# A chunked delta-rule attention beside two matmul layers: attention steps as one TensorE burst each

## The chip, the cores and the metric

The kernel runs on one core of one Trainium2 chip. Its time is the time of one launch in device microseconds (us), inputs and outputs in the chip's main memory. Five instruction queues work side by side: PE (TensorE, with the weight loads shown apart as PEld), DVE (VectorE), ACT (ScalarE), POOL (GpSimd) and SP (SyncE, which issues every data DMA here). Each queue keeps its written order.

## The reference

```python
def _attn_ref(q, k, v, beta):                # 4 x 8 heads, 768 positions, 48 wide
    k_n = k / (norm(k) + 1e-6)
    state = zeros(B, H, 48, 48)
    for t in range(768):
        y[t] = q[t] @ state
        v_old = state.T @ k_n[t]
        state = state + beta[t] * outer(k_n[t], v[t] - v_old)
def _moe_ref(x, w_in, w_out, a, b):          # x [3072, 384], w_in [384, 2048]
    h = x @ w_in
    P = a[0] + a[1]*h + a[2]*h**2 + a[3]*h**3
    Q = 1 + |b[0]| * |h| + |b[1]| * h**2
    return (P / (Q + 1e-6)) @ w_out
def _moe2_ref(x, w_in, w_out):
    return max(x @ w_in, 0)**2 @ w_out
```

The result is `_moe2_ref(_moe_ref(attention))`.

## The kernel before

The 768 positions are cut into 12 chunks of 64, times 4 batches: 48 chunk steps, eight to a group, six groups (`g` = 0 to 5 in the code, here group one to group six). Inside a chunk the recurrence is a triangular inverse, made once for a whole group by POOL or DVE and two rounds of small matmuls (`m1`, L626, and `m2`, L640); `m1` and `m2` read transfers that pass through DRAM (`td`, `nd`). Then each step n does, for all 8 heads of its batch:

- **k**: `kv`, k and state and q, into a PSUM tile H. Two copies with a mask (POOL, L759) give M; the DVE takes a part from `vn` (L764).
- **t**: `tv`, inverse times `vn`, into U; two copies put it into the tile X.
- **c3**: L780 and L781, the output Y; one copy into `xin`.
- **u**: `ku`, k_n times U, added to the state by the DVE (L798).
- **g**: `gram`, the Gram matrix of the step two groups on (groups two to four), one copy into `Gs`.

In the profile k, t, u and g all stand on L721 and are told apart by their operands: `X,kTc`, `vn,TT`, `X,kn`, `kTg`. Before, a step's work stands in three PE tasks (`first`, `rest`): k of step n with t of step n-1; then c3; then u with g.

Layer one has 96 units (six blocks of 512 tokens times 16). **A** (L921) is nine matmuls of a unit into one PSUM bank, held until the rational function (ACT L938, L939, L944, L945, POOL L941, DVE L942 to L948) has read it; **B** (L957) is three calls, six matmul instructions, into three accumulator banks. Layer two, with 96 units more, follows without attention. Counted from one, the attention of group two stands between the units of block one, that of group six between those of block five; block six has none. A block needs the output of the group of its number.

PSUM has 8 banks: 3 accumulators, a pool `h` of 3 for A, a pool `att` of 2 for attention. A planner sets the order: every task has an engine, a planned duration, a due time and its dependences; `Plan.play` lays them out by a list schedule, `Plan.late` sets due times from the end, eight rounds, and the best order is written out. The kernel on the chip has only that order and the waits that follow from the data.

```python
    acc = banks[0:3]
    PL.pool("h", banks[3:6])
    PL.pool("att", banks[6:8])
    pl = ("att",) if g else ("att", "h")
```

Of the kernel before, what the change touches and what calls it, by code (L numbers as in the profile page):

```python
# [242 lines left out]
def kernel(ctx, tc, kT, kS, qT, kn, vn, beta, par_in, w1, w2, outT):  # L243
    nc = tc.nc
    PL = Plan()
    add, slot = PL.add, PL.slot
# [56 lines left out]
    TN = at.tile([128, 8, NP, 32], F32, name="TN")  # L303
# [132 lines left out]
    def gload(n, due, nb=0):  # L436
        dma(128, lambda: slot["kg", n], kS[n], w=[("kg", n)], due=due - 5, nb=nb, alloc=(("kTg",), ("kg", n)))

    def gram(n):

        t, kt = ps(("G", n), [128, NP, C]), slot["kg", n]
        for p in range(NP):
            for j in range(2):
                r = kt[64 * j:64 * j + 48, p]
                yield t[64 * j:64 * j + 64, p], r, r

    def gstore(n, due):
        either(0.37, 0.36, lambda: (slot["Gs", n], ps(("G", n), [128, NP, C])), r=[("G", n)], w=[("Gs", n)], due=due,
            alloc=(("Gs",), ("Gs", n)), free=[("G", n)])
        dma(128, gs[n // 8][:, n % 8], lambda: slot["Gs", n], r=[("Gs", n)], w=[("gs", n)], due=due, free=[("Gs", n)])  # L450

    def attention(g):
# [81 lines left out]
        if g < 2:  # L534
            add("DVE", 2.0, lambda: V.transpose(Gb.rearrange("r q c -> r c q"), Tt.rearrange("p a b -> p b a")), r=["Tt"], w=GB, due=d1, lock=1)
            add("DVE", 2.0, lambda: V.transpose(DN.rearrange("r s p c -> r c (s p)"), Tt), r=["Tt"], w=["DN"], due=d1 + 1, lock=1)
        else:
            dma(512, td[g], Tt, r=["Tt"], w=[("td", g)], due=d1, lat=2.0)
            add("ACT", 2.05, lambda: A_.copy(Gb, Tt.rearrange("p a b -> p b a")), r=["Tt"], w=GB, due=d1)
        TTg = TT[g % 2]  # L540
        if g < 2:
# [8 lines left out]
        for i in (1, 0) if g > 1 else ():  # L550
            for j in range(2):
                o = 64 * j + 32 * i
                dma(128, TTv[o:o + 32, :, 32 * i:32 * i + 32], tdv[i, j], r=[("td", g)], w=[("TTx", g % 2, i, j)],
                    due=d1 + 2, lat=3.4, iss=0.6, after=[PL.last[wT[0]]] if wT[0] in PL.last else [])
        if g > 1:
            for j in range(2):
                dma(128, nd[g][j], Gb[64 * j:64 * j + 32], r=GB, w=[("nd", g, j)], due=d1 + 2)
                for hf in range(2):
                    x = 64 * j + 32 * hf
                    dma(64, TN[x:x + 32, 4 * hf:4 * hf + 4].rearrange("r s p c -> r (s p) c"), nd[g][j][16 * hf:16 * hf + 16].rearrange("q r c -> r q c"),  # L560
                        r=[("nd", g, j)], w=[("TN", hf, x)], due=d1 + 3, lat=3.2, iss=0.6)
                dma(64, TTv[64 * j:64 * j + 32, 16:32, 32:64], tdv[1, j][:, 16:32], r=[("td", g)], w=[("T", g % 2, 1, 64 * j)], due=d1 + 2, lat=3.2, iss=0.6)

# [139 lines left out]
        def ku(k):  # L703

            n = 8 * g + k
            x, t, kn_ = X[n % B], dv(n), KN[n // B % 2]
            for p in range(NP):
                yield t[64:112, p], kn_[0:64, n % B, p], x[0:64, 0, p, 64:112]
                yield t[0:48, p], kn_[64:128, n % B, p], x[64:128, 1, p, 64:112]

        def products(*gens):

            gens = list(gens)
            while gens:
                for q in list(gens):
                    for _ in range(2):
                        y = next(q, None)
                        if y is None:
                            gens.remove(q)
                            break  # L720
                        M.matmul(*y, start=True, stop=True)  # L721

        def yv(n):
            return slot["Y", n][:, 0:NP * C].rearrange("r (p t) -> r p t", p=NP)
# [39 lines left out]
                    V.tensor_tensor(v_[:, b], v_[:, b], ps(hk, [128, NP, 112])[:, :, 64:112], op=ALU.subtract)  # L764
                add("DVE", 0.38, cr, r=[hk], w=[("vn", cb, b)], due=due, free=[hk])

        def rest(k, due):
            n = 8 * g + k
            c, b = divmod(n, B)
            cb, x, uk, yk, dk = c % 2, X[b], ("U", n), ("Y", n), ("dS", n)  # L770
            for j in range(2):
                def uo(j=j):
                    o = 64 * j
                    return x[o:o + 64, j, :, 64:112], ps(uk, [128, NP, D])[o:o + 64]
                either(0.33, 0.33, uo, r=[uk], w=[("Us", b, j)], due=due, free=[uk], after=[PL.last["S", b]] if c == 0 else [])

            def c3():
                t = yv(n)
                for p in range(NP):
                    M.matmul(t[0:48, p], x[0:112, 0, p, 64:112], x[0:112, 0, p, 0:64], start=True, stop=True)  # L780
                    M.matmul(t[64:112, p], x[:, 1, p, 64:112], x[:, 1, p, 0:64], start=True, stop=True)  # L781
            xr = [(y, b, j) for y in ("M", "Us") for j in range(2)]
            add("PE", 0.62, c3, r=xr + [("q", b), ("q1", b), ("S", b)], w=[yk], due=due + 2, alloc=(pl, yk))
            m = n + 16 if 0 < g < NG - 2 else None
            if m:
                gload(m, due)
            add("PE", 0.55, lambda: products(ku(k), *([gram(m)] if m else [])), r=[("Us", b, 0), ("Us", b, 1), ("kn", cb), yk] + ([("kg", m)] if m else []),
                w=[dk] + ([("G", m)] if m else []), due=due + 3, alloc=[(pl, ("G", m))] if m else None, free=[("kg", m)] if m else [])
            if m:
                gstore(m, due + 4)  # L790
# [12 lines left out]
            if b == B - 1:  # L803
                t2 = CT * (c % 2)
                for j, o in ((0, 0), (1, 64)):
                    dma(48, xin[o + 48:o + 64, 0:NK, t2:t2 + CT], xin[o:o + 48, 3, t2:t2 + CT],
                        r=[("xin", c % 2, y) for y in range(B)], w=[("xin3", c % 2, j)], due=due + 7, iss=0.57)

        for k in range(8):
            dn = step_due(8 * g + k)  # L810
            head(k)
            if g:
                first(k, k - 1 if k else None, dn)
                middle(k, dn + 1)
                if k:
                    rest(k - 1, dn + 1)
            else:
# [4 lines left out]
        if g:  # L822
            first(None, 7, dn + 3)
            rest(7, dn + 4)

    def pload():
        SY.dma_start(par[:, 0:6], par_in)
# [276 lines left out]
```

## Time and profile before

| what | value |
|---|---|
| median of 3 runs | 1109.71 us (1107.1 to 1110.93) |
| the profiled execution | 1110.19 us, its span 1108.5 us |
| PE busy | 1057.7 us (95%), 10014 matmuls and as many weight loads |
| DVE, ACT, POOL busy | 703.4, 647.6, 401.2 us |
| layer one's first A | 103.5 us |
| first A of its last block | 626.0 us |

A row of a timeline gives the start, the time from the first start to the last end, the engine, the line, the operation, the tiles, the shape and how many instructions are merged. An idle time before it stands in brackets, with what ended it. A PE row's last instruction is counted to its own end, which the next row may overlap.

### The profile page before, as it was taken

To read this page: it belongs to the slowest core of one execution; us is meant where nothing else is said; L and a number is where in the kernel's file an instruction comes from. 1 tells how busy PE (TensorE), PEld (TensorE's weight loads), DVE (VectorE), ACT (ScalarE), POOL (GpSimd) and SP (SyncE) were. 2 spreads that over 40 slices of the span, in tenths; PEclk is the share of its full clock that TensorE was granted. 3 is DMA by queue.
4 is the path that set the end of the run, shared out by engine and by line. 5 is a ranking of instruction groups with operands and counts; after the bars stand their busy time and mean duration, and the time that the engine had idled before them with its cause. 6 is when DMAs were issued, how large, how long until landed. Compare 5 with 4: busy or idle time off the path is not lost.

```text
span 1108.5 us, 24471 instructions
## 1 busy us (share of the span) xinstructions
PE 1057.7 (95%) x10014; PEld 752.1 (68%) x10014; DVE 703.4 (63%) x1124; ACT 647.6 (58%) x1173; POOL 401.2 (36%) x540
## 2 busy tenths in 40 slices
PE   6588999799989999999999899999999999999998
PEld 5576665466656666666666555688888888888887
DVE  5658889888658768766777599994334343333432
ACT  5264788676767777677778588754333242333422
POOL 6104589569628844972233143551000000000000
PEclk7677899999999999999999999999999999999999
DMA  7455326741650174034010220720001010000000
GB/s 235 120 144 166 75 90 190 166 128 31 144 116 34 50 161 110 5 103 83 29 28 12 90 85 30 252 89 29 29 0 57 1 51 8 1 29 1 29 1 29
DMA packets 120544, 84.01 MB, mean 76 GB/s; under 512 B 88048, under 2 KB 105584, under 8 KB 120432
## 3 DMA queue, kind: packets, MB, share of 16 engines
q1 hardware_dynamic: 120432, 82.44, 26.8%
q8 instruction: 79, 1.29, 0.5%
q14 instruction: 33, 0.27, 0.1%
HBM read 63.41 MB, written 17.83 MB: 73 GB/s over the span
## 4 chain that ended last, share of the span: by engine, by line
PE 84%; DVE 6%; POOL 3%; issue 3%; DMA 3%; ACT 1%; SPq 1%; DVEq 0%; ACTq 0%; POOLq 0%
PE bank L921 33%; PE bank L957 19%; PE bank L983 6%; PE bank L981 6%; PE bank L982 6%; PE bank L721 6%; PE bank L780 2%; PE bank L640 1%; POOL Tt L508 1%; DMA X<-in_qT_dram 1%; PE bank L626 1%; POOL tmp L504 1%; POOL mem L941 1%; PE bank L585 1%; DVE tmp L495 1%
## 5 line engine op out<-in xcount | busy, mean ns | idle before, releaser
L921 PE MATMUL bank<-xh,A 128*128 128x512 f32 x1152 | 360.6, 394 | 1.1 <-POOL A L880 1.1
L957 PE MATMUL bank<-mem,B 128*128 128x512 f32 x576 | 278.7, 615 | 0.7 <-DVE mem L948 0.7
L921 PE MATMUL bank<-xl,A 128*128 128x512 f32 x576 | 256.5, 445 | 6.0 <-DVE mem L948 5.2
L921 PEld LDWEIGHTS bank<-xh,A 128*128 128x128 f32 x1152 | 218.2, 190 | 63.4 <-issue 15.1
L941 POOL TENSOR_TENSOR mem<-mem 128x512 f32<-128x512 f32 x96 | 129.1, 1344 | 202.4 <-ACT mem L939 201.9
L957 PEld LDWEIGHTS bank<-mem,B 128*128 128x128 f32 x576 | 104.3, 192 | 97.5 <-issue 84.3
L969 DVE SCALAR_TENSOR_TENSOR mem<-bank,mem 128x512 f32<-128x512 f32 x96 | 66.3, 690 | 151.3 <-ACT mem L968 151.1
L968 ACT ACTIVATE mem<-bank 128x512 f32<-128x512 f32 x96 | 57.4, 598 | 152.9 <-PE bank L921 151.0
L921 PEld LDWEIGHTS bank<-xl,A 128*128 128x128 f32 x576 | 109.1, 189 | 45.9 <-issue 15.5
L983 PE MATMUL bank<-gh,C 128*128 128x512 f32 x288 | 113.7, 395 | 0.0
L981 PE MATMUL bank<-gl,C 128*128 128x512 f32 x288 | 113.5, 394 | 0.0
L982 PE MATMUL bank<-gh,C 128*128 128x512 f32 x288 | 112.0, 389 | 0.0
L972 DVE TENSOR_TENSOR gl<-mem,gh 128x512 fp32r<-128x512 f32 x96 | 71.5, 745 | 63.3 <-ACT gh L971 63.2
L946 DVE SCALAR_TENSOR_TENSOR mem<-mem,par,bank 128x512 f32<-128x512 f32 x96 | 71.3, 743 | 53.4 <-ACT bank L945 53.2
L971 ACT CAST gh<-mem 128x512 fp32r<-128x512 f32 x96 | 59.6, 621 | 74.8 <-DVE mem L969 62.0
L944 ACT ACTIVATE mem<-mem,par 128x512 f32<-128x512 f32 x96 | 69.3, 722 | 36.0 <-POOL mem L941 35.2
L942 DVE TENSOR_TENSOR mem<-bank,mem 128x512 f32<-128x512 f32 x96 | 65.8, 685 | 31.6 <-ACT mem L347 30.8
L938 ACT ACTIVATE mem<-bank 128x512 f32<-128x512 f32 x96 | 57.1, 595 | 46.1 <-PE bank L921 41.2
L939 ACT ACTIVATE mem<-mem,par 128x512 f32<-128x512 f32 x96 | 78.1, 814 | 2.3
L508 POOL TENSOR_TENSOR Tt<-Tt,tmp 128x31 f32<-128x31 f32 (+15 forms) x124 | 72.4, 584 | 8.2
L943 DVE SCALAR_TENSOR_TENSOR mem<-mem,par,bank 128x512 f32<-128x512 f32 x96 | 71.6, 745 | 3.9 <-ACT mem L938 1.4
L347 ACT COPY X<-bank 64x192 f32<-64x192 f32 (+1 forms) x184 | 62.0, 338 | 18.3 <-DVE vn L764 9.7
(124 smaller groups left out, 1546.4 us busy)
## 6 DMA issues: line engine op xcount, KB each, us to landing
raw<-in_w_dram SPq DMA_DIRECT2D x18, 768.0 KB, 5.5
B<-in_w_dram SPq DMA_DIRECT2D x10, 768.0 KB, 4.8
kTg<-in_kS_dram SPq DMA_DIRECT2D x40, 128.0 KB, 3.3
gs<-Gs SPq DMA_DIRECT2D x40, 128.0 KB, 2.5
kTc<-in_kT_dram SPq DMA_DIRECT2D x40, 128.0 KB, 2.5
X<-in_qT_dram SPq DMA_DIRECT2D x96, 48.0 KB, 2.9
kn<-in_kn_dram SPq DMA_DIRECT2D x12, 384.0 KB, 4.1
vn<-in_vn_dram SPq DMA_DIRECT2D x12, 384.0 KB, 3.6
```

Source lines behind the costliest of these rows:

```text
L508: P_.tensor_tensor(Tt[:, 0:a, s + 1:32], Tt[:, 0:a, s + 1:32], tv, op=ALU.subtract)
L921: M.matmul(h, a, b, start=(k == 0 and m == 0), stop=(k == NK - 1 and m == 2))
L939: add("ACT", 0.83, lambda: A_.activation(b(), a(), AF.Identity, bias=s(4), scale=s(5)), r=[ak, "par"], w=[bk], due=due + 3.3, alloc=(("b", ...
L941: add("POOL", 1.32, lambda: P_.tensor_tensor(b(), b(), a(), op=ALU.mult), r=[ak], w=[bk], due=due + 4.2, lock=1)
L943: add("DVE", 0.75, lambda: V.scalar_tensor_tensor(c(), c(), s(1), h(), op0=ALU.add, op1=ALU.mult), r=[hk, "par"], w=[ck], due=due + 6.3)
L944: add("ACT", 0.72, lambda: A_.activation(a(), b(), AF.Ln, bias=s(6)), r=[bk, "par6"], w=[ak], due=due + 6)
L946: add("DVE", 0.75, lambda: V.scalar_tensor_tensor(c(), c(), s(0), h(), op0=ALU.add, op1=ALU.mult), r=[hk, "par"], w=[ck], due=due + 8)
L957: M.matmul(acc[d], Bw[j][:, 128 * d:128 * d + 128], slot[gk], start=(j == 0), stop=(j == NJ - 1))
L972: add("DVE", 0.72, lambda: V.tensor_tensor(gl(), b(), gh(), op=ALU.subtract), r=[bk, gk, "late"], w=[lk], due=due + 5, lock=1, alloc=(("gl ...
L981: M.matmul(acc[d], wh, gl, start=(j == 0), stop=False)
L982: M.matmul(acc[d], wl, gh, start=False, stop=False)
L983: M.matmul(acc[d], wh, gh, start=False, stop=(j == NJ - 1))
```

## The change

In groups two to six one task `burst(t)` does at once k of step t, t of step t-1, and c3 and u of step t-2 (and g for step t-1): ten bursts a group. H, U and Y may take banks of either pool, and g goes into the free part of U's bank. Group one keeps the old tasks. The planned times of the transfers behind the inverse are longer, which moves only the planned order.

```diff
-    def gram(n):
...
+    def gram(n, t=None):
...
-            dma(512, td[g], Tt, r=["Tt"], w=[("td", g)], due=d1, lat=2.0)
+            dma(512, td[g], Tt, r=["Tt"], w=[("td", g)], due=d1, lat=2.5)
...
-                    due=d1 + 2, lat=3.4, iss=0.6, after=[PL.last[wT[0]]] if wT[0] in PL.last else [])
+                    due=d1 + 2, lat=4.5, iss=0.6, after=[PL.last[wT[0]]] if wT[0] in PL.last else [])
...
+        def burst(t, due):
+            r, w, al, fr, dur = [], [], [], [], 0.0
+            k0, k1, k2 = (x if 0 <= x < 8 else None for x in (t, t - 1, t - 2))
+            m = 8 * g + k1 + 16 if k1 is not None and g < NG - 2 else None
+            if k2 is not None:
+                n, b = 8 * g + k2, k2 % B
+                r += cin(b) + [("kn", n // B % 2)]
+                w, al, dur = w + [("Y", n), ("dS", n)], al + [(("att", "h"), ("Y", n))], dur + 0.65
+            if k0 is not None:
+                n, b = 8 * g + k0, k0 % B
+                r += [("kc", n), ("q", b), ("q1", b), ("S", b)]
+                fr += [("kc", n)]
+                w, al = w + [("H", n)], al + [(("att", "h"), ("H", n))]
+            if k1 is not None:
+                n = 8 * g + k1
...
+                w, al = w + [("U", n)], al + [(("att", "h"), ("U", n))]
+            if m:
+                gload(m, due - 1)
+                r, w, fr = r + [("kg", m)], w + [("G", m)], fr + [("kg", m)]
+            def go():
+                if k2 is not None:
+                    c3(8 * g + k2)
+                products(*([kv(k0)] if k0 is not None else []), *([tv(k1)] if k1 is not None else []),
+                         *([ku(k2)] if k2 is not None else []), *([gram(m, slot["U", m - 16][:, NP * D:NP * (D + C)].rearrange("r (p c) -> r p c", p=NP))] if m else []))
+            q = max((0.76 if k0 is not None else 0) + (0.36 if k2 is not None else 0), (0.37 if k1 is not None else 0) + (0.44 if m else 0))
+            add("PE", 0.22 + dur + q, go, r=r, w=w, due=due, alloc=al, free=fr)
+            if m:
+                gstore(m, due + 2, ("U", m - 16))
...
+        for t in range(10 if g else 0):
+            dn = step_due(8 * g + t) if t < 8 else step_due(8 * g + 7) + 3 * (t - 7)
+            burst(t, dn)
+            if t < 8:
+                middle(t, dn + 1)
+            if 0 < t < 9:
+                ucopy(t - 1, dn + 1)
+            if t > 1:
+                result(t - 2, dn)
```

`ucopy` (two copies of U) and `result` (copy of Y, state add, loads of q) are the rest of the old `rest`, unchanged. PE in the middle of group four (unit 41 of layer one), before; X0 to X3 are the four batches' tiles, L957 is B, L921 is A:

```order
L921 MATMUL bank5_74<-xh2_98,A8_87 128x512 x2
L780 MATMUL bank6_75<-X0_107 48x64
L781 MATMUL bank6_75<-X0_107 48x64
...
L721 MATMUL bank6_75<-X0_107,kn0_128 48x48 x2
L721 MATMUL bank7_76<-kTg0_136 64x64 x2
...
L957 MATMUL bank0_69<-mem_102,B_95 128x512
L721 MATMUL bank7_76<-X2_109,kTc2_134 64x112 x2
L721 MATMUL bank6_75<-vn0_130,TT1_112 64x48 x2
...
L957 MATMUL bank1_70<-mem_102,B_95 128x512
L957 MATMUL bank2_71<-mem_102,B_95 128x512
L921 MATMUL bank3_72<-xl0_99,A9_88 128x512
```

The same place now (A is L966, B L1002, c3 L783 and L784, the others L724):

```order
L966 MATMUL bank5_74<-xh2_98,A8_87 128x512 x2
L783 MATMUL bank6_75<-X0_107 48x64
...
L724 MATMUL bank3_72<-X2_109,kTc2_134 64x112 x2
L724 MATMUL bank7_76<-vn0_130,TT1_112 64x48 x2
L724 MATMUL bank6_75<-X0_107,kn0_128 48x48 x2
L724 MATMUL bank7_76<-kTg1_137 64x64 x2
...
L1002 MATMUL bank0_69<-mem_102,B_95 128x512
L1002 MATMUL bank1_70<-mem_102,B_95 128x512
L1002 MATMUL bank2_71<-mem_102,B_95 128x512
L783 MATMUL bank3_72<-X1_108 48x64
```

Two stretches of small matmuls with a B call between them became one, the burst's third bank is bank 3 of A's pool, and the next burst writes that bank again three B calls later. ACT at that place, before (L347 is the copies; L938, L939, L944, L945 are the rational function):

```order
L347 COPY X2_109<-bank7_76 64x4x64 x2
L347 COPY X1_108<-bank6_75 64x4x48 x2
L944 ACTIVATE mem_102<-mem_102,par_77 128x512
L945 ACTIVATE bank5_74<-mem_102 128x512
L938 ACTIVATE mem_102<-bank3_72 128x512
L347 COPY xin_78<-bank7_76 112x4x64
L939 ACTIVATE mem_102<-mem_102,par_77 128x512
L347 COPY Gs1_139<-bank6_75 128x256
```

And now (L983 and L984 are what L938 and L939 were):

```order
L347 COPY X3_110<-bank7_76 64x4x64 x2
L347 COPY X2_109<-bank4_73 64x4x48 x2
L347 COPY Gs0_138<-bank4_73 128x256
L347 COPY xin_78<-bank3_72 112x4x64
L983 ACTIVATE mem_102<-bank4_73 128x512
L984 ACTIVATE mem_102<-mem_102,par_77 128x512
```

The six copies behind a burst now stand in one piece, with the next unit's first operation behind them.

## Rows read from the trace of the kernel before

**Rows 1.** The page: chain that ended last, by engine.
```profile
PE 84%; DVE 6%; POOL 3%; issue 3%; DMA 3%; ACT 1%; SPq 1%; DVEq 0%; ACTq 0%; POOLq 0%
```

**Rows 2.** Busy time by stretch; the first line names the columns.
```profile
core 0: us, PE busy (x) PEld busy (x) DVE busy (x) ACT busy (x) POOL busy (x), PEclk, DMA share, GB/s
141.00:212.00 71.00, 67.62 (x829) 41.69 (x821) 64.07 (x98) 56.95 (x110) 61.89 (x79) 1.00 0.54 156
526.00:626.00 100.00, 99.80 (x767) 60.58 (x765) 70.42 (x116) 68.73 (x126) 26.91 (x32) 1.00 0.09 28
```

**Rows 3.** PE timeline of one step of group three: kt, t, c3 and ug.
```profile
303.17 0.61 PE L921 MATMUL bank<-xh,A 128*128 128x512 f32 x2
303.72 0.31 PE L721 MATMUL bank<-X,kTc 48*64 48x112 f32 x2
...
304.63 1.98 PE L957 MATMUL bank<-mem,B 128*128 128x512 f32 x4
306.54 0.67 PE L721 MATMUL bank<-vn,TT 64*64 64x48 f32 x16
307.14 0.26 PE L780 MATMUL bank<-X 112*48 112x64 f32 x1
...
311.13 0.61 PE L921 MATMUL bank<-xh,A 128*128 128x512 f32 x2
311.68 0.26 PE L780 MATMUL bank<-X 112*48 112x64 f32 x1
...
312.26 0.25 PE L721 MATMUL bank<-X,kn 64*48 64x48 f32 x2
...
312.88 2.84 PE L957 MATMUL bank<-mem,B 128*128 128x512 f32 x6
```

**Rows 4.** PE timeline, group six: c3 and u without g.
```profile
580.12 0.61 PE L921 MATMUL bank<-xh,A 128*128 128x512 f32 x2
...
581.25 0.56 PE L721 MATMUL bank<-X,kn 64*48 64x48 f32 x16
581.74 1.12 PE L957 MATMUL bank<-mem,B 128*128 128x512 f32 x2
```

**Rows 5.** PE timeline: B with nothing before it; k alone, then B.
```profile
329.80 2.74 PE L957 MATMUL bank<-mem,B 128*128 128x512 f32 x6
...
334.53 0.98 PE L721 MATMUL bank<-X,kTc 48*64 48x112 f32 x16
335.44 2.84 PE L957 MATMUL bank<-mem,B 128*128 128x512 f32 x6
```

**Rows 6.** PE timeline, group three: around a c3 that stands alone.
```profile
246.43 0.61 PE L921 MATMUL bank<-xh,A 128*128 128x512 f32 x2
...
247.56 2.84 PE L957 MATMUL bank<-mem,B 128*128 128x512 f32 x6
```

**Rows 7.** Timeline of all engines behind a kt of group four.
```profile
381.03 1.13 PE L957 MATMUL bank<-mem,B 128*128 128x512 f32 x2
...
381.54 1.44 ACT L347 COPY X<-bank 64x256 f32<-64x256 f32 x4
381.60 0.80 PE L921 MATMUL bank<-xl,A 128*128 128x512 f32 x1
```

**Rows 8.** DVE timeline: the last operation on that unit's bank.
```profile
392.06 0.69 DVE L948 SCALAR_TENSOR_TENSOR mem<-bank,mem 128x512 f32<-128x512 f32 x1
```

**Rows 9.** PE's waits from 141 to 224 us: total, times, longest.
```profile
PE bank L721 <- ACT X L347: 2.0, 1, 2.0
PE bank L921 <- POOL A L880: 1.1, 2, 0.6
```

**Rows 10.** Chain of waits near the end of block one: start, us, what.
```profile
212.85 1.03 POOL A L880
```

**Rows 11.** PE timeline at the m2 of group four.
```profile
323.58 1.39 PE L640 MATMUL bank<-ws,TN 32*32 32x32 f32 x86 [3.02 <-issue]
```

**Rows 12.** The page's instruction queue: packets, MB, share.
```profile
q8 instruction: 79, 1.29, 0.5%
```

More of the change, by code (lines that the diff above doesn't have):

```diff
@@ L437, in gload @@
         dma(128, lambda: slot["kg", n], kS[n], w=[("kg", n)], due=due - 5, nb=nb, alloc=(("kTg",), ("kg", n)))
-    def gram(n):
-        t, kt = ps(("G", n), [128, NP, C]), slot["kg", n]
+    def gram(n, t=None):
+        t, kt = ps(("G", n), [128, NP, C]) if t is None else t, slot["kg", n]
         for p in range(NP):
@@ L445, in gram, with gstore @@
                 yield t[64 * j:64 * j + 64, p], r, r
-    def gstore(n, due):
-        either(0.37, 0.36, lambda: (slot["Gs", n], ps(("G", n), [128, NP, C])), r=[("G", n)], w=[("Gs", n)], due=due,
-            alloc=(("Gs",), ("Gs", n)), free=[("G", n)])
+    def gstore(n, due, u=None):
+        def go():
+            t = ps(("G", n), [128, NP, C]) if u is None else slot[u][:, NP * D:NP * (D + C)].rearrange("r (p c) -> r p c", p=NP)
+            return slot["Gs", n], t
+        either(0.37, 0.36, go, r=[("G", n)], w=[("Gs", n)], due=due,
+            alloc=(("Gs",), ("Gs", n)), free=[u or ("G", n)])
         dma(128, gs[n // 8][:, n % 8], lambda: slot["Gs", n], r=[("Gs", n)], w=[("gs", n)], due=due, free=[("Gs", n)])
@@ L553, in attention @@
                 dma(128, TTv[o:o + 32, :, 32 * i:32 * i + 32], tdv[i, j], r=[("td", g)], w=[("TTx", g % 2, i, j)],
-                    due=d1 + 2, lat=3.4, iss=0.6, after=[PL.last[wT[0]]] if wT[0] in PL.last else [])
+                    due=d1 + 2, lat=4.5, iss=0.6, after=[PL.last[wT[0]]] if wT[0] in PL.last else [])
         if g > 1:
             for j in range(2):
-                dma(128, nd[g][j], Gb[64 * j:64 * j + 32], r=GB, w=[("nd", g, j)], due=d1 + 2)
+                dma(128, nd[g][j], Gb[64 * j:64 * j + 32], r=GB, w=[("nd", g, j)], due=d1 + 2, lat=4.2)
                 for hf in range(2):
@@ L560, in attention @@
                     dma(64, TN[x:x + 32, 4 * hf:4 * hf + 4].rearrange("r s p c -> r (s p) c"), nd[g][j][16 * hf:16 * hf + 16].rearrange("q r c -> r q c"),
-                        r=[("nd", g, j)], w=[("TN", hf, x)], due=d1 + 3, lat=3.2, iss=0.6)
-                dma(64, TTv[64 * j:64 * j + 32, 16:32, 32:64], tdv[1, j][:, 16:32], r=[("td", g)], w=[("T", g % 2, 1, 64 * j)], due=d1 + 2, lat=3.2, iss=0.6)
+                        r=[("nd", g, j)], w=[("TN", hf, x)], due=d1 + 3, lat=5.0, iss=0.6)
+                dma(64, TTv[64 * j:64 * j + 32, 16:32, 32:64], tdv[1, j][:, 16:32], r=[("td", g)], w=[("T", g % 2, 1, 64 * j)], due=d1 + 2, lat=4.8, iss=0.6)
         for hf in range(2 if g < 2 else 0):
@@ L765, in middle, with ucopy @@
                 add("DVE", 0.38, cr, r=[hk], w=[("vn", cb, b)], due=due, free=[hk])
-        def rest(k, due):
+        def ucopy(k, due):
             n = 8 * g + k
             c, b = divmod(n, B)
-            cb, x, uk, yk, dk = c % 2, X[b], ("U", n), ("Y", n), ("dS", n)
+            x, uk = X[b], ("U", n)
             for j in range(2):
@@ L775, in rest, with c3, cin, result @@
                 either(0.33, 0.33, uo, r=[uk], w=[("Us", b, j)], due=due, free=[uk], after=[PL.last["S", b]] if c == 0 else [])
[L777 to L790, printed above, removed]
+        def c3(n):
+            t, x = yv(n), X[n % B]
+            for p in range(NP):
+                M.matmul(t[0:48, p], x[0:112, 0, p, 64:112], x[0:112, 0, p, 0:64], start=True, stop=True)
+                M.matmul(t[64:112, p], x[:, 1, p, 64:112], x[:, 1, p, 0:64], start=True, stop=True)
+        def cin(b):
+            return [(y, b, j) for y in ("M", "Us") for j in range(2)] + [("q", b), ("q1", b), ("S", b)]
+        def result(k, due):
+            n = 8 * g + k
+            c, b = divmod(n, B)
+            x, yk, dk = X[b], ("Y", n), ("dS", n)
             t = CT * (c % 2) + C * b
@@ L807, in rest @@
                         r=[("xin", c % 2, y) for y in range(B)], w=[("xin3", c % 2, j)], due=due + 7, iss=0.57)
+        def rest(k, due):
+            n = 8 * g + k
+            c, b = divmod(n, B)
+            yk, dk = ("Y", n), ("dS", n)
+            ucopy(k, due)
+            add("PE", 0.62, lambda: c3(n), r=cin(b), w=[yk], due=due + 2, alloc=(pl, yk))
+            add("PE", 0.55, lambda: products(ku(k)), r=[("Us", b, 0), ("Us", b, 1), ("kn", c % 2), yk], w=[dk], due=due + 3)
+            result(k, due)
@@ new lines, in burst, with go @@
+        def burst(t, due):
[13 more added lines that the diff above has]
+                n = 8 * g + k1
+                r += [("T", g % 2, k1 // 4, o) for o in (0, 64)] + [("vn", n // B % 2, k1 % B)]
+                r += [("TTx", g % 2, i, j) for i in range(2) for j in range(2)] + ([("TT", g % 2)] if g < 2 else [])
+                w, al = w + [("U", n)], al + [(("att", "h"), ("U", n))]
+            if m:
+                gload(m, due - 1)
+                r, w, fr = r + [("kg", m)], w + [("G", m)], fr + [("kg", m)]
+            def go():
+                if k2 is not None:
[6 more added lines that the diff above has]
+                gstore(m, due + 2, ("U", m - 16))
@@ L809, in attention @@
         for k in range(8):
-            dn = step_due(8 * g + k)
             head(k)
[L812 to L817, printed above, removed]
+            if not g:
+                dn = step_due(8 * g + k)
                 first(k, None, dn)
@@ L821, in attention @@
                 rest(k, dn + 4)
-        if g:
-            first(None, 7, dn + 3)
-            rest(7, dn + 4)
+        for t in range(10 if g else 0):
[7 more added lines that the diff above has]
+                result(t - 2, dn)
     def pload():
```

## The prediction

> **What bounds the kernel now.** First I read the chain of waits: PE carries 84% of it [rows 1]. Then the busy times by stretch. While group six's attention runs (526 to 626 us) PE is busy 99.80 of 100 us and no other engine over 71, so there a microsecond off PE is a microsecond off the end. Between 141 and 212 us, in block one, it is less clear: PE 67.62, but DVE 64.07 and POOL 61.89 of 71 us, because the first layer's weights are prepared there [rows 2]. Then the PE timeline, which shows what small matmuls cost between the large ones; then ACT and DVE behind a step, since the new order asks them to be quicker.
>
> **PE work, before.** Large matmuls of A follow each other at 0.23 us, so a row of two ends its share 0.46 us after its start. From the A row at 303.17 to the B row at 304.63 are 1.46 us; less 0.46 the stretch of k and t costs 1.00 [rows 3]. k alone costs as much: 334.53 to 335.44 is 0.91 from its first matmul to B, and 303.72 to 304.63 is 0.91 too [rows 3, 5]. So t goes beside k for nothing: they use different lanes (k: rows of one half of the array into columns of the other; t: the same half). u shares k's lane, g shares t's. c3 with u and g costs 1.75 - 0.46 = 1.29 [rows 3]; without g 1.62 - 0.46 = 1.16 [rows 4]. c3 alone costs 1.13 - 0.46 = 0.67 [rows 6]; u with g apart 0.62 from first matmul to B, and about 0.09 ahead of it, 0.71 [rows 3]. t ahead of a c3 takes 0.60 [rows 3]. After every stretch the six B instructions take 2.84 instead of 2.74 [rows 5]: 0.10 more per stretch, which I add to each.
>
> A group with g, eight steps: k 1.10, seven kt at 1.10, eight c3+u+g at 1.39, one t 0.60: 20.5 us. Without g (groups five and six): 1.10 + 7.70 + 8 x 1.26 + 0.60 = 19.5.
>
> **PE work, now.** A full burst is c3 and then four kinds in two lanes. Ahead of it 0.09 (311.13 + 0.46 to 311.68); c3 and the step to the next kind 0.58 (311.68 to 312.26) [rows 3]. The longer lane is k then u. The sixteen k take 0.98 [rows 5]; the last one is 0.26 long, so it started at 0.72, and with one spacing of 0.10 the lane is held 0.82; 0.09 more until B. The sixteen u take 0.56 [rows 4], 0.21 of it the last one's: held 0.40. Lane: 0.82 + 0.40 + 0.09 = 1.31. The other lane, t and g, is 0.51 + 0.53 + 0.09 = 1.13 by the same way [rows 3] and hides. Burst: 0.09 + 0.58 + 1.31 + 0.10 = 2.08, with or without g. Bounds: if the lanes only pair as they did before (k beside t, then u beside g) 2.21; if nothing overlaps beyond before, the two old stretches, 2.49 (2.36 without g).
>
> Ten bursts of a group with g: k 1.10; k+t+g 1.32; six full 12.5; c3+t+u+g 1.90; c3+u 1.26: 18.1, so 2.4 less, three times: -7.3. Without g: 1.10 + 1.10 + 12.5 + 1.37 + 1.26 = 17.3, so 2.2 less, twice: -4.4. At five places the order before sets c3 and u further apart (0.77 + 0.81 against 1.39, so 0.2 each); these go: -1.0. PE work: **-12.7 us**, with 2.49 for a burst -2.
>
> **New waits.** Before, a kt had an A or two B calls behind it before its U was needed, and M another stretch more. Now the next burst needs at once the two copies of U, the DVE part of `vn`, and three banks, which the burst before has just filled. Behind the kt that ends at 381.03, ACT starts its four copies at 381.54 and ends at 382.98 [rows 7]: 1.95 us. The new order leaves between two bursts mostly an A and a B or more (2.9 us), or three B calls (2.57: three times 0.86, from [rows 5]), but at five places two B calls or one (1.7 or 0.9). There it is 0.3 us late and once 1.1: some 2 us. With only two banks left to A during the bursts, the next wait is for the rational function: A's start at 381.60 to L948's end at 392.75 is 11.15 us of holding a bank, with copies of a step in between [rows 7, 8]. In group four the new order comes back to the same bank after two A, two bursts and three B calls, 10.8 us: 0.4 late; groups three and six have similar places, some 1.5 us together. Sum **+3.5 us**. Below, zero (the copies may be split with the DVE, which had 30% free); above, if ACT's six copies stand in front of the rational function everywhere, 0.4 at each of 45 gaps, +18.
>
> The Trainium skill's page "TensorEngine Tiling (Array Packing)", section PSUM Bottleneck, speaks against the change: packing speeds up TensorE and not the emptying of PSUM, so the copies may become the bound, and it wants ScalarE and VectorE both on them. By it the +18 would be due; the row of four copies, 1.95 us against gaps of mostly 2.6 or more, bears it out only at the tight places.
>
> **Block one.** PE waits there 3.1 us for a copy and for weights [rows 9]; the last weight's POOL part ends at 213.88 [rows 10], and PE can't pass it, whatever it saves. The DVE has 7 of 71 us free [rows 2]. The order also puts one A of A's first three behind more filler, since a bank of `h` is taken early by H. I take -0.5 for all of this beside the PE work; bounds -4.6 (all of PE's waits and the late unit gone) and +4 (the 3.5 us of PE work of this group saved for nothing).
>
> **Nothing else.** The longer planned times issue no transfer and add no wait; they move `m1` and `m2`, which in the rows are held by no transfer. From the last block on the order is the same on every engine, so what block five gains reaches the end whole.
>
> The sum: -12.7 + 3.5 - 0.5 = -9.7. The profiled execution took 1110.19 us, 0.5 over the median of the runs shown: 1110.2 - 9.7 = **1100.5 us**.
>
> **Rivals.**
> 1. The waits don't come and block one gives its waits back: -12.7 - 4.6 = -17.3, 1093. For: the planner's order already leaves most gaps longer than the copies. Against: the tight places, and DVE in block one.
> 2. Nothing gained, by instruction loading. PE's instructions come in packets of 1.29 MB / 79 [rows 12], for 10014 matmuls and as many weight loads 254 each. In m2 of group four PE stands 3.02 us on "issue" [rows 11], with 256 instructions of m1 just behind it. A full burst is 160 instructions; 254 take at the tightest a burst, two B calls and a good half of the next, 4.8 us, against about 2.7 us in m1 and m2. If a packet needs more than that (3.02 + 2.7 = 5.7), ten places wait 0.9: +9, 1108 or so with the other terms. Against: before, a step's 128 to 160 instructions in 7 us never waited so. The Trainium skill's page "Runtime: NRT & Kernel Launch", section Instruction fetch mechanics, has this loading hidden behind the issue of instructions, so by it this rival is nil; the 3.02 us in m2 say that here it isn't always.
> 3. Slower: the emptying of the banks becomes the bound. Place: between two full bursts; each of 45 gaps waits on the last of the six copies, because an operation of the rational function (0.6 to 0.8 us) stands before them on ACT. Price per gap 0.4: +18, 1110.2 - 12.7 + 18 - 0.5 = 1115. It decides from 0.3 us a gap, where the gain is eaten. For: the order puts six copies in a piece and the next unit's first operation behind them, so A's banks come free later too. Against: in rows 2 ACT has 31 of 100 us free.
> 4. The burst doesn't overlap more than the old pairs did (2.49): -2 + 3.5 - 0.5 = +1, 1111. Against: the equal 0.91 of k alone and k with t.
>
> **How the numbers follow.** Forecast 0.58 (1095 to 1106), rival one 0.18, two 0.11, three 0.09, four 0.04. A run of this kernel tells 0.3%, 3.3 us, from no change. Faster holds the forecast, rival one and a quarter of rival two: 0.79. Same: the rest of two, part of three and four: 0.12. Slower: the rest, 0.09. The range takes rival one in and most of two, 1090 to 1110.
>
> **What would show it.** Full bursts from first matmul to the next large one near 1.9 us; 2.3 or more and the lanes are wrong. PE waits in groups three to six on ACT or DVE of some 3 us; 10 or more and rival three is on. Any "issue" stop inside a burst speaks for rival two. The last block's first A should come at about 616 us instead of 626.0. If the end moves less than that A does, something behind it took the gain back.

## The result and the profile after

The changed kernel takes 1095.84 us (1091.49 to 1099.99, 4 runs) where the kernel before took 1108.4 on the same chip: ratio 0.988 (95% interval 0.984 to 0.992), some 13 us less. The forecast was 1100.5, 9.7 us less than the profiled execution before. A second set of runs (first experiment) gave 0.988 again (0.985 to 0.990). The profiled execution is the fastest of the four: 1091.49 us, its span 1089.8.

The chain that ended last, by engine, from the page of the changed kernel, against [rows 1]:

```profile
PE 76%; DVE 9%; POOL 5%; ACT 3%; issue 3%; DMA 2%; SPq 2%; DVEq 0%; POOLq 0%; ACTq 0%
```

PE still carries it, with less than before. Busy time while group six's attention runs, with the columns of [rows 2]:

```profile
509.00:607.00 98.00, 97.89 (x766) 60.67 (x765) 69.33 (x116) 69.90 (x127) 26.89 (x32) 1.00 0.10 29
```

As in [rows 2] PE is full and no other engine above 72%, so work taken off PE is still worth its length there. Now one full burst of group three on PE, between two B calls (L783 is c3, L724 the other kinds, L1002 is B):

```profile
252.72 1.98 PE L1002 MATMUL bank<-mem,B 128*128 128x512 f32 x4
254.63 0.26 PE L783 MATMUL bank<-X 112*48 112x64 f32 x1
...
255.22 0.31 PE L724 MATMUL bank<-X,kTc 48*64 48x112 f32 x2
255.23 0.32 PE L724 MATMUL bank<-vn,TT 64*64 64x48 f32 x4
...
255.38 0.29 PE L724 MATMUL bank<-kTg 48*64 48x64 f32 x3
255.46 0.20 PE L724 MATMUL bank<-X,kn 64*48 64x48 f32 x1
...
256.35 0.26 PE L724 MATMUL bank<-X,kn 64*48 64x48 f32 x4
256.54 1.13 PE L1002 MATMUL bank<-mem,B 128*128 128x512 f32 x2
```

k and t, then g and u, begin within 0.25 us of each other and all are through 1.32 us after the first of them (255.22 to 256.54). From c3's first matmul to the next B are 1.91 us; with the 0.09 ahead of it the stretch costs 2.00, and the B instructions behind it take the same 0.10 more as in [rows 5] (0.53 us from the first B's start to the second's, where it is 0.43 without a stretch ahead). The forecast had 2.08 in all, the trace 2.10.

The last block's first A, 626.0 us before, on PE's timeline:

```profile
607.42 0.79 PE L966 MATMUL bank<-xl,A 128*128 128x512 f32 x1
```

It comes 18.6 us sooner, and the end 18.7 (1108.5 less 1089.8): from there on nothing is gained or lost. As the profiled execution is the fastest of the four, these 18.7 are more than the 12.6 of the medians. Where those 18.6 come from, by the first A of each block (103.5, 224.2, 327.3, 427.6, 525.9 and 626.0 us before; 102.5, 214.1, 314.1, 413.6, 509.6 and 607.4 now): 1.0 ahead of layer one, 9.1 in block one, 8.5 in blocks two to five. PE's waits in blocks two to five (total, times, longest, us), first the kernel before:

```profile
PE bank L640 <- issue: 4.5, 3, 3.0
PE bank L957 <- DVE mem L948: 0.7, 3, 0.3
PE bank L721 <- ACT X L347: 0.2, 1, 0.2
```

and the changed kernel:

```profile
PE bank L643 <- ACT ws L347: 4.4, 2, 2.3
PE bank L966 <- DVE xl L950: 1.3, 2, 0.7
PE bank L643 <- issue: 1.1, 1, 1.1
PE bank L966 <- DVE mem L993: 0.8, 1, 0.8
PE bank L1002 <- DVE mem L993: 0.6, 2, 0.5
```

No burst waits for a copy. What is new: m2 (L643) waits for the copy of m1's result, 2.3 and 2.1 us. The timeline of all engines at the first of the two says why:

```profile
308.96 0.35 ACT L476 ACTIVATE nby<-Gb,tiny 128x32 f32<-128x32 f32 x1 [3.09 <-DMA Gb<-gs]
...
310.84 0.59 ACT L347 ACTIVATE ws<-bank 128x512 f32<-128x512 f32 x1
...
311.49 1.29 PE L643 MATMUL bank<-ws,TN 32*32 32x32 f32 x128 [2.29 <-ACT ws L347]
```

ACT stands 3.09 us on a load for the next group's inverse (`Gb` from `gs`); the rational function and the copy `ws` queue behind it, and PE behind the copy.

### The profile page after: what moved, and what is told of

Its sections match the earlier page's. It is cut to its first block, busy times and chain, and to the rows that moved or that the text cites. A ratio compares the mean times of both kernels' runs of the same rounds, so it can differ in the third digit from the quotient of the medians.

```text
span 1089.8 us, 24429 instructions
## 1 busy us (share of the span) xinstructions
PE 1037.7 (95%) x10022; PEld 748.8 (69%) x10022; DVE 700.5 (64%) x1122; ACT 645.8 (59%) x1175; POOL 400.0 (37%) x540
## 4 chain that ended last, share of the span: by engine, by line
PE 76%; DVE 9%; POOL 5%; ACT 3%; issue 3%; DMA 2%; SPq 2%; DVEq 0%; POOLq 0%; ACTq 0%
PE bank L966 31%; PE bank L1002 16%; PE bank L1028 6%; PE bank L1026 6%; PE bank L1027 6%; PE bank L724 5%; SPq L332 2%; PE bank L783 2%; POOL Tt L511 2%; POOL tmp L507 2%; POOL mem L986 1%; DVE raw L910 1%; DMA kTg<-in_kS_dram 1%; DVE mem L993 1%; DVE mem L987 1%
## 5 line engine op out<-in xcount | busy, mean ns | idle before, releaser
L966 PE MATMUL bank<-xh,A 128*128 128x512 f32 x1152 | 358.2, 392 | 0.9 <-POOL A L925 0.9
L1002 PE MATMUL bank<-mem,B 128*128 128x512 f32 x576 | 271.5, 605 | 0.6 <-DVE mem L993 0.6
L966 PE MATMUL bank<-xl,A 128*128 128x512 f32 x576 | 254.8, 442 | 8.5 <-DVE mem L993 6.7
L966 PEld LDWEIGHTS bank<-xh,A 128*128 128x128 f32 x1152 | 217.3, 189 | 61.1 <-issue 14.5
L1002 PEld LDWEIGHTS bank<-mem,B 128*128 128x128 f32 x576 | 106.0, 191 | 99.4 <-issue 86.8
L966 PEld LDWEIGHTS bank<-xl,A 128*128 128x128 f32 x576 | 108.6, 189 | 53.4 <-issue 12.7
L1028 PE MATMUL bank<-gh,C 128*128 128x512 f32 x288 | 113.8, 395 | 0.0
L983 ACT ACTIVATE mem<-bank 128x512 f32<-128x512 f32 x96 | 56.9, 592 | 44.8 <-PE bank L966 39.0
L984 ACT ACTIVATE mem<-mem,par 128x512 f32<-128x512 f32 x96 | 78.0, 813 | 2.4
L347 ACT COPY X<-bank 64x256 f32<-64x256 f32 (+1 forms) x186 | 62.6, 339 | 20.2 <-DVE vn L767 9.6
L511 POOL TENSOR_TENSOR Tt<-Tt,tmp 128x31 f32<-128x31 f32 (+15 forms) x124 | 69.9, 563 | 8.3
```

The source lines that it names most:

```text
L511: P_.tensor_tensor(Tt[:, 0:a, s + 1:32], Tt[:, 0:a, s + 1:32], tv, op=ALU.subtract)
L966: M.matmul(h, a, b, start=(k == 0 and m == 0), stop=(k == NK - 1 and m == 2))
L984: add("ACT", 0.83, lambda: A_.activation(b(), a(), AF.Identity, bias=s(4), scale=s(5)), r=[ak, "par"], w=[bk], due=due + 3.3, alloc=(("b", ...
L1002: M.matmul(acc[d], Bw[j][:, 128 * d:128 * d + 128], slot[gk], start=(j == 0), stop=(j == NJ - 1))
L1028: M.matmul(acc[d], wh, gh, start=False, stop=(j == NJ - 1))
```

## The experiments

All were timed beside the kernel before, and each ratio is to that kernel on the same chip. "Block one" below is the time from its first A to that of block two, "two to five" from there to the first A of the last block, each from the profiled execution. The fifth column is the time lost at half clock within block one: the sum over 2 us windows of the window times (1 - granted clock). It is what the lower clock cost only if PE would not have waited instead. Columns four to six come from one execution of each kernel.

| kernel | median us | ratio (95% interval) | block one | of it half clock | two to five |
|---|---|---|---|---|---|
| before (first trace) | 1109.71 | 1 | 120.7 | 7.7 | 401.8 |
| changed (first trace) | 1095.84 | 0.988 (0.984-0.992) | 111.6 | 1.7 | 393.3 |
| e1 changed, again | 1096.48 | 0.988 (0.985-0.990) | 112.2 | 2.0 | 395.5 |
| e2 longer times alone | 1113.12 | 1.003 (1.001-1.005) | 122.2 | 7.5 | 400.2 |
| e3 bursts, old times | 1103.06 | 0.993 (0.990-0.996) | 121.5 | 2.7 | 391.9 |
| e4 bursts from group three | 1107.05 | 0.998 (0.996-1.000) | 120.1 | 3.8 | 395.8 |
| e5 lanes in pairs | 1097.13 | 0.988 (0.986-0.990) | 113.8 | 1.7 | 394.0 |
| e6 c3 last | 1097.82 | 0.988 (0.986-0.990) | 113.4 | 1.7 | 393.2 |
| e7 copies on ACT | 1097.36 | 0.988 (0.986-0.990) | 114.1 | 2.2 | 395.0 |
| e8 two banks for A | 1126.9 | 1.016 (1.013-1.018) | 121.1 | 9.4 | 396.3 |
| e9 Gram load 7.0 | 1105.68 | 0.996 (0.994-0.997) | 118.9 | 8.5 | 394.7 |
| e10 Gram load 5.0 | 1106.8 | 0.996 (0.995-0.998) | 120.6 | 5.1 | 394.3 |
| e11 before, Gram load 7.0 | 1112.32 | 1.002 (1.000-1.004) | 116.2 | 1.7 | 403.0 |
| e12 c3 twice | 1098.73 | 0.991 (0.988-0.994) | 113.0 | 0.4 | 394.9 |

**e1, the changed kernel again** (no edit).

> The changed kernel once more, for the spread of its times and for the same-chip comparison. Theory one (the time comes from PE work: a step's two stretches of small matmuls, some 1.1 + 1.3 to 1.4 us, became one of 2.10): ratio 0.985 to 0.992; a full burst again 2.00 us plus 0.10, and the blocks two to five of layer one again within 1.5 us of 100.0, 99.5, 96.0 and 97.8 us. Theory two (a good part of the 18.7 us by which its first trace was shorter is TensorE's granted clock, which that trace shows at half speed for some 6 us less of the first 640 us than the trace of before): the span differs from 1089.8 us by the time spent at half clock in this trace.

Ratio 0.988, the full burst 2.00 us again, blocks two to five 100.9, 100.4, 96.4 and 97.8 us. Theory one holds. Theory two holds from layer one on at most: the four blocks are 2.2 us longer than in the first trace, with 5.1 us lost at half clock against 1.7 there. Over the whole execution it fails: the mean granted clock is higher here (0.974 against 0.970), and the span is 5.4 us longer, 2.5 of them ahead of layer one, whose first A comes at 105.0 instead of 102.5.

**e2, the longer planned times alone**, in the kernel before (the five `lat` of the diff):

```diff
-            dma(512, td[g], Tt, r=["Tt"], w=[("td", g)], due=d1, lat=2.0)
+            dma(512, td[g], Tt, r=["Tt"], w=[("td", g)], due=d1, lat=2.5)
```

> The kernel before, with the longer planned times of the transfers and nothing else. Theory one (the bursts make the gain, the planned times none): 1105 to 1111 us, ratio 0.997 to 1.003. Rival (the order around the inverse makes it: m1 and m2 moved to where their operands are ready): 1104 us or less, ratio 0.996 or less, and less waiting at m1 and m2 (7.8 us of gaps in the trace of before).

1113.12, two us above theory one's range and slightly slower than the kernel before (1.003). The rival, 1104 or less, falls; the planned times by themselves gain nothing.

**e3, the bursts with the old planned times** (the same five undone in the changed kernel):

```diff
-            dma(512, td[g], Tt, r=["Tt"], w=[("td", g)], due=d1, lat=2.5)
+            dma(512, td[g], Tt, r=["Tt"], w=[("td", g)], due=d1, lat=2.0)
```

> The changed kernel with the planned transfer times of before. Theory one: within 3 us of the changed kernel, 1093 to 1099 us. Rival (the longer times matter with bursts, where m1 and m2 find fewer stretches to stand between): 4 us or more above the changed kernel, with waits of m1 or m2 on a transfer or a copy that it doesn't have.

The rival's number came, 6.6 us above e1, but not at m1 or m2: blocks two to five are the shortest of all, 391.9, and block one is 121.5. The longest of PE's waits there:

```profile
PE bank L966 <- DVE xl L950: 7.2, 1, 7.2
```

and on ACT, ahead of the copies that the next block's first A needs:

```profile
221.41 0.35 ACT L476 ACTIVATE nby<-Gb,tiny 128x32 f32<-128x32 f32 x1 [6.97 <-DMA Gb<-gs]
```

The load that makes m2 late in the changed kernel makes the whole next block late here. With the longer times SP begins to issue the four transfers of that load 101.9 us after layer one's first A (102.5 to 204.4 us), with the old ones 107.2 us after it (105.8 to 213.0). In blocks two to five m2 waits for `ws` here too, with the old planned times:

```profile
PE bank L643 <- ACT ws L347: 3.7, 2, 2.4
```

So that wait comes with the order of the bursts and not with the longer times; e2, old tasks with the longer times, has none there.

**e4, bursts from group three on** (group two by the old tasks):

```diff
+        def rest0(k, due):
...
+            if g == 1:
...
+                first(k, k - 1 if k else None, dn)
...
-        for t in range(10 if g else 0):
+        for t in range(10 if g > 1 else 0):
```

(`rest0` is the old `rest`.)

> Bursts in groups three to six alone; group two, between the units of block one, keeps the old tasks. Theory one with block one's own gain real (in the traces block one became 9.1 us shorter, of which some 3 us are half clock; 5.2 us attention stretches and 1.3 us waits): 5 to 7 us above the changed kernel, 1100 to 1103 us, blocks two to five as in the changed kernel. Rival (block one is held by the preparing of the weights, so PE work there is worth nothing, and its 9 us were clock and luck): within 2 us of the changed kernel.

1107.05, above both ranges: block one is back at 120.1 (3.8 of it half clock), and blocks two to five keep their gain but for 2.5 us against the first trace of the changed kernel (0.3 against e1). The rival falls. But the order of block one is new here too, so this doesn't tell the old tasks from the new order.

**e5, the lanes in pairs**:

```diff
-                products(*([kv(k0)] if k0 is not None else []), *([tv(k1)] if k1 is not None else []),
-                         *([ku(k2)] if k2 is not None else []), ...
+                products(*([kv(k0)] if k0 is not None else []), *([tv(k1)] if k1 is not None else []))
+                products(*([ku(k2)] if k2 is not None else []), ...
```

> The changed kernel with the same order of tasks; inside a burst k and t are issued to their end and only then u and g, instead of all four in turn. Theory one (part of the gain is that u starts in k's lane and g in t's without a common stop): a full burst 2.11 instead of 2.00 us, 30 of them, 3.5 us in all: 1098 to 1102 us, the four last attention blocks 0.6 to 0.9 us longer each. Rival (the whole gain is that two stretches became one, with one entry and one 0.10 us behind it): 2.00 to 2.03 us a burst and the changed kernel's time, 1094 to 1098 us.

The rival holds: 1097.13 us, and the burst, on PE's timeline:

```profile
260.22 0.26 PE L783 MATMUL bank<-X 112*48 112x64 f32 x1
...
261.53 0.26 PE L724 MATMUL bank<-X,kTc 48*64 48x112 f32 x2
261.55 0.22 PE L724 MATMUL bank<-kTg 48*64 48x64 f32 x2
261.62 0.21 PE L724 MATMUL bank<-X,kn 64*48 64x48 f32 x2
...
262.13 1.13 PE L1002 MATMUL bank<-mem,B 128*128 128x512 f32 x2
```

1.91 us from c3 to B, as with all four in turn: g starts beside the last k, without a stop. So the order in which the four kinds are issued is worth nothing; what gains is that k and t, and c3, u and g, are one stretch: 1.10 + 1.40 = 2.50 became 2.10. By the prediction's terms, 0.28 of these 0.40 are one way in (0.09), one way out (0.09) and one 0.10 less. The other 0.12 would be that g, longer than u, no longer stands alone at the end; no run takes these apart.

**e6, c3 at the end of the burst**:

```diff
             def go():
-                if k2 is not None:
-                    c3(8 * g + k2)
                 products(...)
+                if k2 is not None:
+                    c3(8 * g + k2)
```

> The changed kernel with the same order of tasks; c3 stands at the end of a burst instead of its head, so H and U are ready some 0.6 us sooner and Y later. Theory one (in blocks two to five no burst waits for a copy: the traces show no gap ahead of one there): the same PE work, blocks two to five as before, block one 0 to 3 us shorter (bursts wait there 1.8 to 3.2 us): 1093 to 1098 us. Rival three of the prediction (the copies behind a burst set the pace): 4 us or more gained, 1092 or less.

1097.82, the same time, blocks two to five 393.2. That H and U are ready 0.6 us sooner is worth nothing; block one is not shorter either, so theory one holds but for its hope for block one, and rival three's 1092 or less did not come.

**e7, every copy of a burst on ACT**:

```diff
-                either(0.38, 0.36, co, r=[hk], w=[("M", b, j)], due=due, free=[hk])
+                (cact if g else either)(0.38, 0.36, co, r=[hk], w=[("M", b, j)], due=due, free=[hk])
```

(the copies of U and Y likewise; `cact` adds the copy to ACT alone).

> The changed kernel with every copy of M, U and Y of groups two to six on ACT; the planner may no longer give some to the DVE, and lays out its order anew. Rival three of the prediction (emptying the banks is the bound where ACT does it all): 0.4 us at each of 45 gaps, 1108 to 1116 us, with PE waits on ACT ahead of bursts in blocks two to five. Theory one (the gaps between bursts are longer than the copies): 1094 to 1104 us, no such waits in blocks two to five; what changes is block one, whose order is new.

1097.36. PE's waits in blocks two to five (L969 is A, L1005 B and L724 the small matmuls here; the 2.0 in the first row is ahead of the first A of block two):

```profile
PE bank L969 <- DVE xl L953: 2.8, 2, 2.0
PE bank L1005 <- DVE mem L996: 2.5, 2, 1.6
PE bank L643 <- ACT ws L347: 2.5, 1, 2.5
PE bank L643 <- issue: 1.4, 2, 0.7
PE bank L724 <- ACT xin L752: 0.2, 1, 0.2
```

A burst waits for a copy once, for 0.2 us. Rival three of the prediction falls.

**e8, three banks for attention and two for A**:

```diff
-    PL.pool("h", banks[3:6])
-    PL.pool("att", banks[6:8])
+    PL.pool("h", banks[3:5])
+    PL.pool("att", banks[5:8])
...
```

(the bursts take from `att` alone).

> The changed kernel with three banks kept for attention and two for A, instead of two and three with the bursts free to take from either. The fillers ahead of layer one stop 6 planned us sooner. A unit holds its bank 10.2 us with nothing beside it and up to 13.4 us among steps, so with two banks the units can't follow each other closer than 5.1 us, against 4.65 now. Theory (the shared third bank is what makes bursts affordable: A needs it between the groups): 50 or so of the units of layer one 0.5 us and more later each, 1120 to 1150 us. Rival (A hardly uses its third bank): 1095 to 1105 us.

1126.9: the theory's time, in another place. Blocks two to five are within 3 us of the changed kernel; block one is 9.5 longer (9.4 of it half clock, against 1.7), and the last block, which has no attention, took 98.8 instead of 81.6 us. The longest of its waits, for a bank of A:

```profile
PE bank L966 <- DVE mem L993: 15.4, 7, 5.0
```

against this in the changed kernel:

```profile
PE bank L966 <- DVE mem L993: 5.2, 2, 3.6
```

In blocks two to five A nearly does without its third bank: it waits 6.0 us for a bank there instead of 0.8, and the blocks are only 3 us longer. A unit comes there every 6.2 us on average (396.3 us for 64 units), where the last block of the changed kernel brings one every 5.1 (81.6 for 16). In the last block A can't do without it.

**e9 and e10, the load of the Gram matrices planned longer** (7.0 and 5.0):

```diff
-                    dma(128, Gb[o:o + 32], gv[j, i, :, :, 32 * i:32 * i + 32], lat=3.8, iss=0.6,
+                    dma(128, Gb[o:o + 32], gv[j, i, :, :, 32 * i:32 * i + 32], lat=7.0, iss=0.6,
```

> The changed kernel, with the load of a group's Gram matrices (Gb from gs) planned at 7.0 us instead of 3.8, so that ACT's first operation on it (L476) is put later in its queue. In the trace of the changed kernel ACT stands 7.8 us on this load in three places, and at two of them PE's m2 waits 2.3 and 2.1 us for a copy queued behind it; the trace of before has no such wait. Theory (this is a wait that the new order brought in, and it costs 4 us): 1090 to 1094 us, the m2 waits gone, blocks two and three 1.5 to 2.5 us shorter. Rival (m2 then waits for something else, or the order elsewhere changes as much): 1095 us or more.

> The same with 5.0 us planned for this load. Theory: part of it, 1091 to 1096 us, the waits of ACT on the load some 1.2 us shorter each. Rival (any new order moves block one by several us, whatever the edit): block one off by 3 us or more from the 112 us of the changed kernel, in one direction or the other.

Both theories fail: 1105.68 and 1106.8. e9's rival holds. In e9 ACT no longer waits for the load, and of m2's waits for `ws` 0.4 us are left, but m2 now stands on "issue", its own instructions, as in the kernel before. PE's waits from 103 to 510 us:

```profile
PE bank L643 <- issue: 5.5, 3, 2.1
...
PE bank L643 <- ACT ws L347: 0.4, 1, 0.4
```

Blocks two to five are 394.7 and 394.3, no better than the rest; block one grew to 118.9 and 120.6 (8.5 and 5.1 of it half clock). e10's rival is borne out: a new order moves block one by several us.

**e11, the kernel before with the Gram load at 7.0** (e9's line):

```diff
-                    dma(128, Gb[o:o + 32], ... lat=3.8, iss=0.6,
+                    dma(128, Gb[o:o + 32], ... lat=7.0, iss=0.6,
```

> The kernel before, with 7.0 us planned for the load of the Gram matrices. Its trace shows no wait of ACT on it, so theory: 1106 to 1112 us, blocks two to five within 1 us of 103.1, 100.3, 98.3 and 100.1 us, block one within 3 us of 120.7. Rival (block one's 9 us come from its order alone, and any edit that sets it anew may bring them without a burst): block one at 115 us or less.

1112.32, ratio 1.002; block four is 99.8, 1.5 off its old length, the other three within 1. Block one is 116.2, with 1.7 us of half clock instead of 7.7: shorter by 4.5, but not by a changed task. That is between theory (within 3 us) and rival (115 or less). The time gains nothing by it: layer one starts 2.7 us later in this trace, and block four and the last block are longer.

**e12, c3 twice in group two's bursts**, so that PE has more to do in block one, at the same order:

```diff
-                if k2 is not None:
+                for _ in range((2 if g == 1 else 1) if k2 is not None else 0):
                     c3(8 * g + k2)
```

> The changed kernel with the same order of tasks; in group two, whose bursts stand between the units of block one, the sixteen matmuls of c3 are issued twice (the second time over the same values), eight times some 0.55 us of PE work, 4.4 us in all. Theory (block one's length is set by the order of several engines, not by PE's work, so the 2.8 us of work that bursts took away in this group are little of its 9 us): 1096 to 1099 us, block one 111 to 115 us. Rival (PE's work counts fully there, as in blocks two to five): 1100 to 1103 us, block one 116 to 118 us, blocks two to five as in the changed kernel by either.

The burst is 0.44 us longer (2.35 instead of 1.91 from c3 to B):

```profile
177.84 0.26 PE L783 MATMUL bank<-X 112*48 112x64 f32 x1
...
180.19 0.70 PE L1002 MATMUL bank<-mem,B 128*128 128x512 f32 x1
```

Eight times that is 3.5 us. Block one, with the columns of [rows 2]:

```profile
107.10:220.10 113.00, 107.33 (x1814) 72.84 (x1811) 101.22 (x161) 92.31 (x170) 82.13 (x107) 1.00 0.56 148
```

113.0 us lies in the theory's range and among the 111.6 to 113.8 of the other four kernels of this order, so the rival's 116 to 118 did not come. But that is not PE's work counting for nothing. This trace lost 0.4 us at half clock where the four lost 1.7 to 2.0; with that taken off, it is 112.6 against their 109.9 to 112.1, 0.5 to 2.7 longer. And PE was idle 5.7 us (113.00 - 107.33) where it was idle 6.4 to 8.4 in the four, so part of the added work went into waits. The time, 0.991 (0.988 to 0.994), can be told neither from e1's 0.988 (0.985 to 0.990) nor from e1 with 3.5 us more, 0.991. So PE's work may count there in part; how much, this run doesn't show.

## Why the prediction was right

**The sum.** Forecast -9.7; by the medians -12.6 in the first runs and -13.9 in e1 (1110.33 to 1096.48). The attention work and the waits came out near the forecast; what was missing is a term of block one, TensorE's clock.

**Blocks two to five: right in size.** By the forecast these four groups lose 10.2 us of PE work (2.4 twice, 2.2 twice, and the 1.0 of the five places where c3 and u stood apart, all of which lie in groups three, four and six), and 3.5 come back in waits: -6.7. In the traces the attention stretches and the 0.10 behind each sum to 82.0 us before and 70.2 after, -11.8; the blocks are 8.5 us shorter in the first trace and 6.3 in e1. In the first trace 3.3 came back: PE's waits rose from 5.4 to 8.2 us (the rows above), and 0.5 is not placed. Over all kernels the gain is steady whatever the order: 400.2 to 403.0 us in the three with old tasks there, 391.9 to 396.3 in the eleven with bursts.

**The cost of a burst: right, one bound wrong.** 2.08 forecast, 2.10 measured. The bound of 2.21 (lanes only in pairs) supposed a stop between the pairs; e5 shows none. Rival four (2.49, no overlap beyond before) falls with the 2.10.

**The waits: near in sum, wrong in place.** The forecast put 2 us on copies at the tight places and 1.5 on A's banks. The copies cost nothing (no such wait in blocks two to five, e6, e7). Of the 2.8 us more of waits, A's wait for a bank is 0.8 and the wait for `xl` 1.3; B's wait for the rational function's result is 0.6 against 0.7. The largest, 4.4, is m2 behind ACT's wait on the Gram load, where the forecast had no wait at all. It took the place of 3.4 us of "issue" at m2 (4.5 to 1.1), so m2's balance is +1.0. That the sum was near is partly luck.

**Block one: the mis-sized term.** Forecast -0.5 beside group two's 2.4 of PE work: -2.9. (The bound of +4 took 3.5 us of PE work for this group; the prediction's own sum gives it 2.4.) Measured -9.1, and -8.5 in e1. Block one before, with the columns of [rows 2]:

```profile
103.50:224.20 120.70, 112.66 (x1691) 72.44 (x1689) 102.89 (x161) 93.20 (x172) 85.02 (x110) 0.94 0.50 131
```

and after:

```profile
102.50:214.10 111.60, 104.89 (x1695) 69.36 (x1684) 100.26 (x162) 90.64 (x169) 81.48 (x107) 0.98 0.57 145
```

PE was idle 8.0 us before and 6.7 after (length less busy time): -1.3. Of its busy time 7.7 and 1.7 us are the loss at half clock: -6.0. The rest of its busy time went from 105.0 to 103.2: -1.8. In e1 the three are -1.6, -5.7 and -1.2. So work and waits gave 3.1 and 2.8, which is the forecast's size, and the term that failed is the clock, which the forecast put at nothing by leaving it out. The split supposes that at full clock PE would not have waited longer; no run shows that.

Where the clock was at half, before (the second row is what stood ahead of the third):

```profile
103.50:108.50 5.00, 5.00 (x15) 3.94 (x13) 2.25 (x5) 2.90 (x5) 0.00 (x0) 0.50 0.36 140
126.00:128.00 2.00, 0.74 (x73) 0.63 (x63) 2.00 (x4) 1.39 (x4) 1.81 (x2) 1.00 0.22 33
129.00:135.90 6.90, 6.90 (x76) 3.41 (x66) 5.89 (x10) 4.61 (x8) 6.04 (x13) 0.51 0.04 6
214.30:217.80 3.50, 3.50 (x48) 2.36 (x50) 2.31 (x5) 0.60 (x1) 0.41 (x1) 0.51 0.98 154
```

and after, the one place:

```profile
129.50:133.00 3.50, 3.50 (x5) 1.17 (x4) 3.39 (x6) 2.98 (x5) 3.19 (x6) 0.51 0.02 5
```

The first stretch before is the end of one that began ahead of layer one. Ahead of the next PE idled 1.26 of 2 us, and then ran nearly 7 us at half speed.

One more thing differs, the end of the chain. Before, the last weight's first operation on ACT stands behind the copies of the last step. The chain of waits of the kernel before, in order of time, up to [rows 10]:

```profile
205.05 0.23 PE bank L780
...
205.70 0.65 PE bank L721 x26
...
207.11 0.37 ACT xin L347
207.48 0.84 ACT raw L863
208.34 1.95 DVE raw L865
...
212.32 0.47 ACT A L879
```

Group two's last c3 (L780) starts at 205.05 there; in the changed kernel, on PE's timeline:

```profile
193.73 0.26 PE L783 MATMUL bank<-X 112*48 112x64 f32 x1
...
194.32 0.56 PE L724 MATMUL bank<-X,kn 64*48 64x48 f32 x16
```

11.3 us sooner, since a step now takes one place among the units and not two, and the weights come sooner too. The last weight's POOL part, which the forecast took as a wall at 213.88 that PE can't pass, ends at 207.13:

```profile
206.12 1.01 POOL L925 TENSOR_TENSOR A<-raw,A 128x384 fp32r<-128x384 f32 x1 [3.04 <-ACT A L924]
```

How much of block one's gain belongs to the bursts isn't shown. With the loss at half clock taken off, block one is 113.0 to 116.3 us in the four kernels with old tasks in group two (before, e2, e4, e11) and 109.9 to 112.6 in the five of the changed order. But it is 110.4 to 118.8 in the other orders with bursts there (e3, e7, e8, e9, e10), so bursts alone don't bring the gain.

**The rivals.** Two (instruction loading): "issue" stays at m2; ahead of or inside bursts it takes 0.8 us before layer one, 0.2 in block one and nothing later, where the rival had 9. Three (copies as the bound): fell. The Trainium skill's page "TensorEngine Tiling (Array Packing)", section PSUM Bottleneck, says that copying out of PSUM may become the bottleneck once tiling has made TensorE four times as fast; here, where two stretches of 2.50 us became one of 2.10, it did not, even with ACT alone (e7). One (-17.3): the first trace was near it, -18.7, but not for its reason, since the waits came; the medians were not near it.

**What stays open.** What in block one decides how long PE falls to half clock wasn't isolated, and of the kernel before there is one trace: whether each of its executions loses 7.7 us there isn't known. The mean clocks of its 67 executions beside the experiments warn against counting every such us: they run from 0.958 to 0.975, which is 28 to 47 us lost per execution, and the time rose by only 0.23 us for each us lost (a straight line through the 67). In the trace 30 of 41 us are lost ahead of layer one, so this doesn't settle block one. Nothing tried is faster than the changed kernel.

## What to carry to other kernels

Small matmuls between large ones were paid here by the stretch as well as by the matmul: merge stretches first, and don't spend effort on the order inside one. Where one engine is full for a whole block, count its work; where several queues are nearly full, a change of order can be worth more than the work it saves, in either direction, so time the order by itself before crediting the work, and split a block's change into idle time, clock and work. A wait taken out of a list schedule can come back under another name at the same instruction, as m2's did in e9: look at the sum.

## What the runs showed of the hardware

Small matmuls of four kinds in two lanes, issued in turn or in pairs one after the other, take the same 1.91 us from c3's first matmul to the next B (the changed kernel and e5). A stretch of small matmuls costs 0.09 us ahead of it and makes the large ones behind it 0.10 us longer, in both kernels. The second sixteen matmuls of c3 cost 0.44 us (e12), where the first take 0.59 with the step to the next kind (254.63 to 255.22). PE at half clock for nearly 7 us followed 1.26 us of idling within 2 us (126 to 128 us of the kernel before), in the middle of the program.
